# Decode attention with a cached window and a bilinear GLU: x by two rows on ScalarE's queue, and the first weights and K in one load

## The chip, the cores and the metric

The kernel runs on one core of one Trainium2 chip. The metric is the device time of one execution in microseconds, the median of the runs. The profile is one further execution, read by a hardware profiler.

## What is computed

One decoding step for two sequences (B = 2, one token each, D = 512). The input is normalized and goes two ways, and both are added to it:

```python
xn = layernorm(x)
# attention over the last W = 2048 positions of the cache, 32 heads of 128
q = xn @ wq                          # [B, 32, 128]
p = softmax(q . k * 128 ** -0.5)     # k, v: the cache's last 2048 positions
a = (p @ v) @ wo
# GLU without a nonlinearity, F = 1376
f = ((xn @ w_gate) * (xn @ w_up)) @ w_down
y = x + a + f
```

All arrays are float32. K and V of the window are 2 x 32 x 2048 x 128 values each, 67 MB for K and as much for V; with the weights the kernel reads 159 MB for each token pair.

## The kernel before

**The stream.** Everything large lies in one array, `stream`, in the order in which it is needed. `blocks()` (L45) writes that order out: a list of steps, each a list of fields. A field is K of one head with its share of wq (`k`, `wq`), V of one head with its rows of wo (`v`, `wo`), a half of the gate and up weights (`wg`, `wu`), or rows of w_down (`wd`, `wr`). A step holds up to three units of K or V, some 7 MB, as 128 partitions of up to 13,824 words. `pump()` (L143) issues the loads, all on SP's queue, into a ring of three buffers; `done()` (L166) counts the uses of a step's fields, and when the last is done the buffer goes to the next step. SP's issue of that step then waits for the engines that read the old one.

**The small first load.** Ahead of the steps stands a load of 542 words for each partition, into a tile `first` of its own that takes no buffer of the ring: x already laid out by column (`x`, 8 words), the two selection matrices `pick` and `rows` (16 and 6 words), and the part of wq that belongs to head 0 (`w` 0, 512 words). After the three steps that fit the ring SP issues two more small loads: `x_nat`, 16 rows of 128 words with x in the layout of the output, and `carry`, a 9 x 9 matrix that moves accumulator rows.

**Layer norm and projection.** DVE sums x, TensorE spreads the sum over the partitions by a matmul with `mean_w`, the same for the variance, ACT takes the root, and DVE writes `xnb`, the normalized x broadcast over 128 columns (L216 to L234). `project_first(0)` (L245) makes q of head 0 from `w` 0 and `project_first(1)` q of heads 1 to 3 from `w` 1; `project_q` makes the later ones, four heads at a time, while K of earlier heads is used.

**One head.** `products` multiplies K with q on DVE (128 x 4096 words), `sums` adds over the head's 128 columns on DVE, `maxima` and `weights` make the softmax with GpSimd and ACT, `pv` multiplies with V on TensorE into `o_ps`, ACT copies that out, `transpose` turns it with `pick`, ACT scales it into `oT`, and `project_o` adds its product with wo to the accumulator `acc`.

**The accumulator.** `oT` and `hT` have M = 9 columns, of which columns 0 and 8 hold the two sequences (RB = 8), so sequence b stands on accumulator row 8b. The other columns are set to zero once, at the start. For the last heads the 512 columns are split over four row groups of 32 (`accumulate`, L317). The old accumulator is brought there by a matmul of its copy `acc_sb` with `carry` (L496). At the end DVE adds `x_nat` to it (L529), and the 128 x 128 result goes out.

The engines' instructions stay in the order in which they are written (`InOrder`); since that helper records every instruction, nearly all carry line 98 in the profile and are told apart by their tiles.

Of the kernel before, what the change touches and what calls it, by code (L numbers as in the profile page):

```python
# [8 lines left out]
F32 = mybir.dt.float32  # L9
AF = mybir.ActivationFunctionType  # L10
ALU = mybir.AluOpType
# [5 lines left out]
P = 128  # L17
B, D, H, DH, SK, F = 2, 512, 32, 128, 8192, 1376
W = min(4096, max(256, SK // 4))
J = W // P  # L20
NC = D // P
FB = 4 * P
NFB = -(-F // FB)
NFC = F // P
FR = F - NFC * P
FH = [(0, 2 * FB), (2 * FB, F)]
LAG = 3
RB = 8
M = RB * (B - 1) + 1
OUT = P  # L30

CARRY = 72
HG = 4
GC = HG * DH
JG = J // 4
CK, CQ, CO = B * J * DH, NC * GC, D
CP = CQ // NC
UNIT = CK + max(CP, CO)
STEP = 3 * UNIT
WD = [(0, 2), (2, 4), (4, 7), (7, NFC - 1), (NFC - 1, NFC)]  # L40
NS = 3
FX = FR // NS


def blocks():  # L45

    def wd(n):
        return [("wd", i, D) for i in range(*WD[n])]

    def k(h):
        return [("k", h, CK)] + ([("wq", h, CP)] if h + HG < H else [])

    def v(h):  # L60
        return [("v", h, CK), ("wo", h, CO)]

    def gu(half):
        n = NC * (FH[half][1] - FH[half][0])
        return [("wg", half, n), ("wu", half, n)]

    units = []
    for h in range(LAG, H - 1):
        units += [k(h), v(h - LAG)]
    ones = [("pick", 0, 8 * B), ("rows", 0, NFB * B)]  # L70
    first = [("x", 0, B * NC)] + ones + [("w", 0, NC * DH)]
    loads = [[("w", 1, CQ - NC * DH)] + k(0) + k(1), gu(0) + k(2)]
    loads += [gu(1) + units[0] + units[1] + wd(0) + [("wr", 0, NS * P)]]
    loads += [sum(units[i : i + 3], []) for i in range(2, len(units), 3)]
    loads += [k(H - 1) + v(H - 1 - LAG) + wd(1)]
    out = [(("f", 0), first)] + [(("s", i), fields) for i, fields in enumerate(loads)]
    late, last = ("s", len(loads)), ("s", len(loads) + 1)
    out += [(late, v(H - 3)), (late, v(H - 2)), (last, [("v", H - 1, CK)])]
    out += [(last, [("wo", H - 1, CO)] + wd(2))]
    return out + [(last, wd(n)) for n in range(3, len(WD))]  # L80
# [33 lines left out]
def kernel(  # L114
    ctx: ExitStack,
    tc: tile.TileContext,
    x_rows: bass.AP,
    carry_rows: bass.AP,
    stream: bass.AP,
    out: bass.AP,  # L120
):
    nc = tc.nc
    pe, dve, act, sp = (InOrder(tc, e) for e in (nc.tensor, nc.vector, nc.scalar, nc.sync))
    SCALE = float(DH) ** -0.5
    BUFS = 3
# [13 lines left out]
    held = 0  # L139
# [3 lines left out]
    def pump():  # L143
        nonlocal held
        while todo:
            key, fields, at = todo[0]
            if key not in tiles:
                if key[0] == "f":
                    n = sum(w for _, _, w in fields)
                    tiles[key] = const.tile([P, n], F32, name="first")  # L150
                elif held == BUFS:
                    return
                else:
                    held += 1
                    tiles[key] = steps.tile([P, STEP], F32, name="step")
                used[key] = 0
            todo.pop(0)
            c0 = used[key]
            for kind, i, w in fields:
                got[kind, i] = (tiles[key][:, used[key] : used[key] + w], key)  # L160
                used[key] += w
            c1 = used[key]
            src = stream[at : at + P * (c1 - c0)].rearrange("(p i) -> p i", p=P)
            sp.dma_start(tiles[key][:, c0:c1], src)

    def done(kind, i):  # L166
        nonlocal held
        _, key = got.pop((kind, i))
        left[key] -= 1
        if left[key] == 0 and key[0] != "f":  # L170
            del tiles[key]
            held -= 1
            pump()

    pump()
    xT = got["x", 0][0].rearrange("p (b c) -> p b c", b=B)
    pick = got["pick", 0][0].rearrange("p (r s b) -> p r s b", s=2, b=B)
    rows = got["rows", 0][0]

    x_nat = const.tile([P, P], F32, name="x_nat")  # L180
    dve.memset(x_nat, 0.0)
    sp.dma_start(x_nat[::RB, :], x_rows)

    carry = const.tile([P, CARRY], F32, name="carry")[:M, :M]
    sp.dma_start(carry, carry_rows)

    mean_w = const.tile([P, P], F32, name="mean_w")
    dve.memset(mean_w, 1.0 / D)
# [16 lines left out]


    oT_ring = [const.tile([P, M], F32, name=f"oT{i}") for i in range(4)]
    for t in oT_ring:
        nc.gpsimd.memset(t, 0.0)


    tr = ps_c.tile([P, 4 * P], F32, name="tr")
    st = const.tile([P, 4, B], F32, name="st")
    xc = const.tile([P, B, NC], F32, name="xc")
    sq = const.tile([P, B, NC], F32, name="sq")
    dve.tensor_reduce(st[:, 0, :], xT, axis=AX.X, op=ALU.add)  # L216
    pe.matmul(tr[:, 0:B], mean_w, st[:, 0, :], start=True, stop=True)
    dve.tensor_tensor(
# [13 lines left out]
    dve.tensor_copy(  # L232
        xnb, xn.rearrange("p c b -> p (c b)").unsqueeze(2).to_broadcast([P, NC * B, P])
    )  # L234

    q_ps, s_t, mm_t, p_t, sum_t, rec_t, o_sbs, oT = {}, {}, {}, {}, {}, {}, {}, {}
    n_acc = bank = 0
# [108 lines left out]
    def transpose(heads, o_sb):  # L346
        d = tr[:, 8 + 4 * bank : 12 + 4 * bank]
        s0, s1 = side(heads[0]), side(heads[-1]) + 1
        dst = d.rearrange("p (s b) -> p s b", b=B)[:, s0:s1, :]
        for r in range(4):  # L350
            pe.matmul(
                dst, o_sb[:, r * DH : (r + 1) * DH], pick[:, r, s0:s1, :],
                start=(r == 0), stop=(r == 3),
            )
        for h in heads:
            rec = rec_t.pop(h)
            oT[h] = oT_ring[h % 4]
            for b in range(B):
                c = B * side(h) + b
                act.activation(  # L360
                    oT[h][:, RB * b : RB * b + 1], d[:, c : c + 1], AF.Copy,
                    scale=rec[:, b : b + 1],
                )

# [23 lines left out]


    hT = const.tile([P, 4, NFB, M], F32, name="hT")  # L390
    dve.memset(hT, 0.0)

    hX = const.tile([P, NS, M], F32, name="hX")
    dve.memset(hX, 0.0)

    def project_gu(half):
        lo, hi = FH[half]
# [12 lines left out]
    def gate():  # L410
        g_sb = small.tile([P, FB], F32, name="o_sb", bufs=2)
        act.copy(g_sb, gu_ps[0])
        h_sb = small.tile([P, FB], F32, name="o_sb", bufs=2)
        dve.tensor_tensor(h_sb, g_sb, gu_ps[1], op=ALU.mult)
        for i in range(4):
            t = tr[:, P + i * P // 2 : P + i * P // 2 + NFB * B]
            pe.matmul(t, h_sb[:, i * P : (i + 1) * P], rows, start=True, stop=True)
            act.copy(hT[:, i, :, ::RB], t.rearrange("p (n b) -> p n b", b=B))
        for i in range(NS):
            t = tr[:, P + (2 * i + 1) * P // 4 : P + (2 * i + 1) * P // 4 + NFB * B]  # L420
            f = (NFC % 4) * P + i * FX - FR
            pe.matmul(t, h_sb[:, f : f + P], rows, start=True, stop=True)
            act.copy(hX[FR:, i, ::RB], t[FR:, (NFB - 1) * B :])

    def down(n):
        for c in range(*WD[n]):
# [62 lines left out]
    down(1)  # L489

    acc_sb = const.tile([M, D], F32, name="acc_sb")
    dve.tensor_copy(acc_sb, acc)
    sums(h + 1)
    transpose([HF], o_sb)
    keep_busy(256)
# [30 lines left out]
    down(3)  # L526
    down(4)
    o_out = const.tile([P, P], F32, name="o_out")
    dve.tensor_tensor(o_out, acc_g, x_nat, op=ALU.add)  # L529

    sp.dma_start(out, o_out[:OUT, :])

# [1 line left out]
def laid_out(x):  # L534
# [1 line left out]
    import numpy as np  # L536

    a = x["A_x"].reshape(B, D)
    first = {
        kind: np.zeros((P, w), a.dtype) for kind, _, w in blocks()[0][1][:3]  # L540
    }
    carry = np.zeros((M, M), a.dtype)
    first["x"][:] = a.reshape(B, P, NC).transpose(1, 0, 2).reshape(P, B * NC)
    for b in range(B):
        for r in range(4):
            for s in range(2):
                first["pick"][8 * s + 4 * b + r :: 32, (2 * r + s) * B + b] = 1.0
        for n in range(NFB):
            first["rows"][32 * n + b, n * B + b] = 1.0
        carry[RB * b, RB * b] = 1.0  # L550
    cache = {
        kind: x[name][:, :, SK - W :, :].reshape(B, H, P, J * DH).transpose(1, 2, 0, 3)
        for kind, name in (("k", "A_k_cache"), ("v", "A_v_cache"))
# [8 lines left out]
    rest = wd[NFC * P :].reshape(FR, NS + 1, P)  # L562

    def field(kind, i):
        if kind in first:
            return first[kind]
        if kind in ("k", "v"):
            return cache[kind][i].reshape(P, CK)
        if kind == "w":
            return (wq[0][:, :, DH:] if i else wq[0][:, :, :DH]).reshape(P, -1)  # L570
        if kind == "wq":
            return wq[i // HG + 1][:, i % HG, :]
        if kind == "wo":
            return wo[i]
        if kind == "wr":
            last = rest[:, NS, :].reshape(NS, FX, P).swapaxes(0, 1)
            return np.concatenate([rest[:, :NS, :], last]).reshape(P, NS * P)
        if kind == "wd":
            return wd[i * P : (i + 1) * P]
        return gu[kind][:, :, FH[i][0] : FH[i][1]].reshape(P, -1)  # L580
# [2 lines left out]
        np.concatenate([field(kind, i) for kind, i, _ in fields], axis=1).ravel()  # L583
        for _, fields in blocks()
    ]
    x_rows = np.zeros((D // P, 32 // RB, P), a.dtype)
    x_rows[:, :B] = a.reshape(B, D // P, P).transpose(1, 0, 2)
    return {
        "x_rows": x_rows.reshape(-1, P),
        "carry": carry,  # L590
        "stream": np.concatenate(parts),
    }

# [31 lines left out]
```

## Time and profile before

| what | value |
|---|---|
| median of 3 runs | 377.54 us (377.41 to 377.73) |
| profiled execution, span from first to last instruction | 375.7 us |
| median less that span | 1.84 us |
| bytes read | 159.47 MB |
| mean rate over the span | 425 GB/s |
| busy, PE / DVE / ACT / POOL | 256.5 / 294.6 / 58.7 / 25.3 us |

The profile holds the span of the profiled execution, not a device time of its own; the median of the runs stands beside it. The rows of the profile name an engine, an operation, the tile written and the tiles read, with start and duration in microseconds; `128*9` in a matmul is the shape of the stationary operand. PEld is TensorE's load of weights, SPq the queue of SP. "DMA share" in a table of windows is the mean busy share of the 16 DMA engines; a packet is counted where it starts, so a short window can show more than 1.

### The profile page before, as it was taken

To read this page: it belongs to the slowest core of one execution; us is meant where nothing else is said; L and a number is where in the kernel's file an instruction comes from. 1 tells how busy PE (TensorE), PEld (TensorE's weight loads), DVE (VectorE), ACT (ScalarE), POOL (GpSimd) and SP (SyncE) were. 2 spreads that over 40 slices of the span, in tenths; PEclk is the share of its full clock that TensorE was granted. 3 is DMA by queue.
4 is the path that set the end of the run, shared out by engine and by line. 5 is a ranking of instruction groups with operands and counts; after the bars stand their busy time and mean duration, and the time that the engine had idled before them with its cause. 6 is when DMAs were issued, how large, how long until landed. Compare 5 with 4: busy or idle time off the path is not lost.

```text
span 375.7 us, 2891 instructions
## 1 busy us (share of the span) xinstructions
PE 256.5 (68%) x1100; PEld 88.1 (23%) x1100; DVE 294.6 (78%) x147; ACT 58.7 (16%) x259; POOL 25.3 (7%) x78
## 2 busy tenths in 40 slices
PE   3396696986548487864848676485867639637996
PEld 3241122331112122211222211121212213021334
DVE  3299691998599499769949976994996799599960
ACT  1021001122020211201112020111202011121131
POOL 1001000000000000100000100000000000000010
PEclk9796988899696966859686786976669887556999
DMA  8999999899999999999999999999999999999995
GB/s 327 463 436 454 408 426 471 383 465 432 414 465 394 459 424 424 461 400 453 418 437 449 412 447 424 432 442 430 436 436 424 437 434 436 436 425 424 419 421 226
DMA packets 4382, 159.70 MB, mean 425 GB/s; under 512 B 514, under 2 KB 658, under 8 KB 1042
## 3 DMA queue, kind: packets, MB, share of 16 engines
q1 hardware_dynamic: 4370, 159.54, 98.5%
q8 instruction: 8, 0.13, 0.1%
q14 instruction: 4, 0.03, 0.0%
HBM read 159.47 MB, written 0.07 MB: 425 GB/s over the span
## 4 chain that ended last, share of the span: by engine, by line
DMA 62%; DVE 29%; PE 7%; ACT 1%; issue 0%; SPq 0%; DVEq 0%
DMA step<-in_stream_dram 62%; DVE s L98 14%; DVE step L98 14%; PE o_ps L98 3%; PE q L98 2%; PE acc L98 2%; PE tr L98 1%; DVE m L98 0%; ACT o_sb L98 0%; ACT oT L98 0%; SPq L98 0%; DVE rec L98 0%; DVE o_out L98 0%; DVEq L98 0%
## 5 line engine op out<-in xcount | busy, mean ns | idle before, releaser
L98 DVE TENSOR_TENSOR step<-step,q 128x4096 f32<-128x4096 f32 x31 | 136.6, 4408 | 53.3 <-DMA step<-in_stream_dram 53.3
L98 PE MATMUL q<-step,xnb 128*128 128x512 f32 (+1 forms) x128 | 92.7, 874 | 75.5 <-DMA step<-in_stream_dram 75.5
L98 DVE TENSOR_REDUCE s<-step 128x32 f32<-128x4096 f32 x32 | 141.4, 4419 | 1.1
L98 PE MATMUL o_ps<-step,p 128*16 128x512 f32 (+1 forms) x512 | 69.7, 682 | 10.3 <-DMA step<-in_stream_dram 10.3
L98 PEld LDWEIGHTS q<-step,xnb 128*128 128x128 f32 x128 | 32.2, 275 | 128.9 <-DMA step<-in_stream_dram 79.1
L98 PE MATMUL acc<-step,oT 128*9 128x512 f32 (+1 forms) x88 | 35.2, 554 | 9.3 <-ACT oT L98 8.1
L98 PE MATMUL tr<-first,o_sb 128*128 128x2 f32 (+2 forms) x198 | 27.6, 258 | 15.3 <-ACT o_sb L98 12.8
L98 ACT COPY o_sb<-o_ps 128x512 f32<-128x512 f32 (+1 forms) x24 | 13.8, 576 | 143.1 <-PE o_ps L98 143.1
L98 PEld LDWEIGHTS tr<-first,o_sb 128*128 128x128 f32 x198 | 25.5, 196 | 37.3 <-ACT o_sb L98 32.6
L295 POOL PARTITION_ALL_REDUCE mm<-m x32 | 11.3, 354 | 283.4 <-DVE rec L98 178.9
L98 PEld LDWEIGHTS o_ps<-step,p 128*16 128x16 f32 x512 | 13.5, 106 | 70.4 <-issue 55.2
L98 ACT ACTIVATE nm<-mm 128x2 f32<-128x2 f32 x32 | 6.5, 203 | 129.5 <-POOL mm L295 129.5
L98 ACT ACTIVATE p<-s,nm 128x16 f32<-128x16 f32 x64 | 19.2, 300 | 1.0
L98 ACT ACTIVATE oT<-tr,rec 128x1 f32<-128x1 f32 x64 | 12.2, 260 | 28.3 <-PE tr L98 28.3
L311 POOL PARTITION_ALL_REDUCE sum<-rs x32 | 12.7, 398 | 54.8 <-ACT p L98 54.8
L98 PE MATMUL o_ps<-step,xn 128*2 128x512 f32 (+1 forms) x48 | 12.9, 593 | 0.0
L98 ACT ACTIVATION_READ_ACCUMULATOR p<-s,nm 128x1 f32 x64 | 12.0, 187 | 0.0
L98 DVE TENSOR_TENSOR step<-step,tr 128x4096 f32<-128x4096 f32 x1 | 4.4, 4421 | 9.3 <-DMA step<-in_stream_dram 9.3
L98 PEld LDWEIGHTS acc<-step,oT 128*9 128x9 f32 x88 | 4.3, 91 | 19.5 <-ACT oT L98 13.1
L98 PE MATMUL q<-xnb,mean_w 128*128 128x512 f32 (+1 forms) x18 | 8.5, 563 | 0.0
L98 PE MATMUL acc<-step,hT 128*9 128x128 f32 (+2 forms) x58 | 7.9, 357 | 0.0
L98 DVE TENSOR_REDUCE m<-s 128x2 f32<-128x32 f32 x32 | 5.9, 186 | 1.1
(43 smaller groups left out, 36.5 us busy)
## 6 DMA issues: line engine op xcount, KB each, us to landing
step<-in_stream_dram SPq DMA_DIRECT2D x16, 6912.0 KB, 33.7
step<-in_stream_dram SPq DMA_DIRECT2D x2, 6400.0 KB, 32.6
step<-in_stream_dram SPq DMA_DIRECT2D x1, 6720.0 KB, 45.6
step<-in_stream_dram SPq DMA_DIRECT2D x1, 6656.0 KB, 28.9
step<-in_stream_dram SPq DMA_DIRECT2D x1, 5376.0 KB, 15.4
step<-in_stream_dram SPq DMA_DIRECT2D x1, 4864.0 KB, 30.1
step<-in_stream_dram SPq DMA_DIRECT2D x2, 2304.0 KB, 17.2
step<-in_stream_dram SPq DMA_DIRECT2D x1, 2048.0 KB, 15.9
```

The lines of the kernel that those rows point to most:

```text
L98: made = call(*args, **kwargs)
L295: nc.gpsimd.partition_all_reduce(mm, m, P, bass_isa.ReduceOp.max)
L311: nc.gpsimd.partition_all_reduce(sum_t[h], rs, P, bass_isa.ReduceOp.add)
```

## The change

- The small first load goes. Its selection matrices (now one field `ones`) and head 0's part of wq stand at the head of the first step, ahead of `w` 1 and K of heads 0 and 1. That step has 11,286 words for each partition, where it had 10,752.
- x comes as `x_own`, two rows of 512 words with a 2 x 2 unit matrix beside them, by a load that ScalarE issues as its first instruction. Four small matmuls with that unit matrix turn it into `xT`, which DVE copies out of PSUM; the layer norm goes on from there.
- ACT copies `pick` and `rows` from the first step into a tile of their own (`ones`), so that the step's buffer can be given back.
- M is 2: `oT` and `hT` have one column for each sequence, there is nothing to set to zero, and accumulator row b is sequence b. `x_nat` and the separate `carry` are gone, with their loads; `carry` is the unit matrix that came with x.
- x is added to the accumulator where it is copied to `acc_sb`, on two rows; the last step on DVE is a copy of `acc_g`.

On SP's queue the three steps that fit the ring are now the first three instructions, and the next one is the load that waits for the first buffer. ACT's queue begins with the load of x. On PE the projection of head 0 waits for the first step.

```diff
-RB = 8
-M = RB * (B - 1) + 1
+M = B
...
-    ones = [("pick", 0, 8 * B), ("rows", 0, NFB * B)]
-    first = [("x", 0, B * NC)] + ones + [("w", 0, NC * DH)]
-    loads = [[("w", 1, CQ - NC * DH)] + k(0) + k(1), gu(0) + k(2)]
+    first = [("ones", 0, ONES), ("w", 0, NC * DH), ("w", 1, CQ - NC * DH)]
+    loads = [first + k(0) + k(1), gu(0) + k(2)]
...
-    out = [(("f", 0), first)] + [(("s", i), fields) for i, fields in enumerate(loads)]
+    out = [(("s", i), fields) for i, fields in enumerate(loads)]
...
+    x_own = const.tile([P, D + M], F32, name="x_own")[:M, :]
+    act.dma_start(x_own, x_rows)
+    x_own, carry = x_own[:, :D].rearrange("m (c p) -> m c p", c=NC), x_own[:, D:]
+
     pump()
-    xT = got["x", 0][0].rearrange("p (b c) -> p b c", b=B)
...
-    x_nat = const.tile([P, P], F32, name="x_nat")
-    dve.memset(x_nat, 0.0)
-    sp.dma_start(x_nat[::RB, :], x_rows)
-
-    carry = const.tile([P, CARRY], F32, name="carry")[:M, :M]
-    sp.dma_start(carry, carry_rows)
...
+    xT = const.tile([P, B, NC], F32, name="xT")
+    for c in range(NC):
+        pe.matmul(tr[:, 16 + B * c : 16 + B * c + B], x_own[:, c, :], carry, start=True, stop=True)
+    dve.tensor_copy(xT, tr[:, 16 : 16 + B * NC].rearrange("p (c b) -> p b c", b=B))
     dve.tensor_reduce(st[:, 0, :], xT, axis=AX.X, op=ALU.add)
...
+    act.copy(ones, got["ones", 0][0])
+    done("ones", 0)
...
-    dve.tensor_copy(acc_sb, acc)
+    dve.tensor_tensor(
+        acc_sb.rearrange("m (p c) -> m p c", c=NC), acc.rearrange("m (p c) -> m p c", c=NC),
+        x_own.rearrange("m c p -> m p c"), op=ALU.add,
+    )
...
-    dve.tensor_tensor(o_out, acc_g, x_nat, op=ALU.add)
+    dve.tensor_copy(o_out, acc_g)
```

More of the change, by code (lines that the diff above doesn't have):

```diff
@@ L27 @@
 LAG = 3
-RB = 8
-M = RB * (B - 1) + 1
+M = B
 OUT = P
-CARRY = 72
 HG = 4
@@ L42 @@
 FX = FR // NS
+ONES = 8 * B + NFB * B
 def blocks():
@@ L117 @@
     x_rows: bass.AP,
-    carry_rows: bass.AP,
     stream: bass.AP,
@@ L147, in pump @@
             if key not in tiles:
[L148 to L151, printed above, removed]
+                if held == BUFS:
                     return
-                else:
-                    held += 1
-                    tiles[key] = steps.tile([P, STEP], F32, name="step")
+                held += 1
+                tiles[key] = steps.tile([P, STEP], F32, name="step")
                 used[key] = 0
@@ L169, in done @@
         left[key] -= 1
-        if left[key] == 0 and key[0] != "f":
+        if left[key] == 0:
             del tiles[key]
@@ L173, in done @@
             pump()
+    x_own = const.tile([P, D + M], F32, name="x_own")[:M, :]
+    act.dma_start(x_own, x_rows)
+    x_own, carry = x_own[:, :D].rearrange("m (c p) -> m c p", c=NC), x_own[:, D:]
     pump()
-    xT = got["x", 0][0].rearrange("p (b c) -> p b c", b=B)
-    pick = got["pick", 0][0].rearrange("p (r s b) -> p r s b", s=2, b=B)
-    rows = got["rows", 0][0]
-    x_nat = const.tile([P, P], F32, name="x_nat")
-    dve.memset(x_nat, 0.0)
-    sp.dma_start(x_nat[::RB, :], x_rows)
-    carry = const.tile([P, CARRY], F32, name="carry")[:M, :M]
-    sp.dma_start(carry, carry_rows)
+    ones = const.tile([P, ONES], F32, name="ones")
+    pick = ones[:, : 8 * B].rearrange("p (r s b) -> p r s b", s=2, b=B)
+    rows = ones[:, 8 * B :]
     mean_w = const.tile([P, P], F32, name="mean_w")
@@ L207 @@
     oT_ring = [const.tile([P, M], F32, name=f"oT{i}") for i in range(4)]
-    for t in oT_ring:
-        nc.gpsimd.memset(t, 0.0)
     tr = ps_c.tile([P, 4 * P], F32, name="tr")
@@ L360, in transpose @@
                 act.activation(
-                    oT[h][:, RB * b : RB * b + 1], d[:, c : c + 1], AF.Copy,
+                    oT[h][:, b : b + 1], d[:, c : c + 1], AF.Copy,
                     scale=rec[:, b : b + 1],
@@ L390 @@
     hT = const.tile([P, 4, NFB, M], F32, name="hT")
-    dve.memset(hT, 0.0)
     hX = const.tile([P, NS, M], F32, name="hX")
-    dve.memset(hX, 0.0)
     def project_gu(half):
@@ L417, in gate @@
             pe.matmul(t, h_sb[:, i * P : (i + 1) * P], rows, start=True, stop=True)
-            act.copy(hT[:, i, :, ::RB], t.rearrange("p (n b) -> p n b", b=B))
+            act.copy(hT[:, i, :, :], t.rearrange("p (n b) -> p n b", b=B))
         for i in range(NS):
@@ L422, in gate @@
             pe.matmul(t, h_sb[:, f : f + P], rows, start=True, stop=True)
-            act.copy(hX[FR:, i, ::RB], t[FR:, (NFB - 1) * B :])
+            act.copy(hX[FR:, i, :], t[FR:, (NFB - 1) * B :])
     def down(n):
@@ L538, in laid_out @@
     a = x["A_x"].reshape(B, D)
[L539 to L543, printed above, removed]
+    ones = np.zeros((P, ONES), a.dtype)
     for b in range(B):
@@ L546, in laid_out @@
             for s in range(2):
-                first["pick"][8 * s + 4 * b + r :: 32, (2 * r + s) * B + b] = 1.0
+                ones[8 * s + 4 * b + r :: 32, (2 * r + s) * B + b] = 1.0
         for n in range(NFB):
-            first["rows"][32 * n + b, n * B + b] = 1.0
-        carry[RB * b, RB * b] = 1.0
+            ones[32 * n + b, 8 * B + n * B + b] = 1.0
     cache = {
@@ L564, in field @@
     def field(kind, i):
-        if kind in first:
-            return first[kind]
+        if kind == "ones":
+            return ones
         if kind in ("k", "v"):
@@ L585, in laid_out @@
     ]
-    x_rows = np.zeros((D // P, 32 // RB, P), a.dtype)
-    x_rows[:, :B] = a.reshape(B, D // P, P).transpose(1, 0, 2)
     return {
-        "x_rows": x_rows.reshape(-1, P),
-        "carry": carry,
+        "x_rows": np.concatenate(
+            [a.reshape(B, P, NC).swapaxes(1, 2).reshape(B, D), np.eye(M, dtype=a.dtype)], axis=1
+        ),
         "stream": np.concatenate(parts),
@@ L623 @@
     y = r.results[0]["out_0_dram"]
-    return y[[32 * g + RB * b for b in range(B) for g in range(D // P)]].reshape(B, 1, D)
+    return y[[32 * g + b for b in range(B) for g in range(D // P)]].reshape(B, 1, D)
```

## The prediction

> **What bounds the kernel now.** I read the page first (share of the engines, DMA queues), then the chain that ended last, then busy time by windows, then the first 75 us of the timeline and the SP queue, then the tail.
>
> ```profile
> span 375.7 us, 2891 instructions
> q1 hardware_dynamic: 4370, 159.54, 98.5%
> DMA 62%; DVE 29%; PE 7%; ACT 1%; issue 0%; SPq 0%; DVEq 0%
> ```
>
> The second line is the load queue: its packets occupied the 16 DMA engines for 98.5% of the whole span. The third is the chain that ended last; its 29% of DVE must not be read as a bound by DVE, since a piece of it ends each time in a load that had long been queued behind others. The windows decide it (columns: stretch, length, busy time of PE, PEld, DVE, ACT, POOL, granted clock, DMA share, GB/s):
>
> ```profile
> 0.00:1.70 1.70, 0.00 (x0) 0.00 (x0) 0.78 (x4) 0.98 (x1) 1.17 (x14) 1.00 0.00 0
> 1.70:2.82 1.12, 0.00 (x0) 0.00 (x0) 0.99 (x3) 0.30 (x1) 0.08 (x3) 1.00 0.87 197
> ...
> 15.60:371.30 355.70, 250.18 (x1032) 82.80 (x1036) 290.68 (x131) 56.84 (x256) 24.09 (x64) 0.79 1.00 432
> 371.30:372.20 0.90, 0.90 (x44) 0.80 (x37) 0.00 (x0) 0.30 (x2) 0.00 (x0) 1.00 0.35 134
> 372.20:374.00 1.80, 0.75 (x24) 0.21 (x12) 0.29 (x1) 0.00 (x0) 0.00 (x0) 1.00 0.00 0
> ```
>
> Between 15.6 and 371.3 us the DMA share is 1.00 at 432 GB/s, while DVE is busy 290.68 of 355.70 us and PE less. The kernel is one uninterrupted stream: 159.54 MB at 432 GB/s are 369.3 us. Around it stand 1.7 us before the first byte, a slow start, and about 3.5 us after the last (372.2 to 375.7). A change moves the time if it moves the start of the stream, its bytes or rate, its tail, or if it lets the queue run dry.
>
> The span is 375.7 us and the median of the runs 377.54; the 1.84 us around the span are taken as unchanged, so a change of the span is carried over to the median one for one. Measurement of this kernel can tell about 0.2%, 0.75 us, from no change.
>
> **The loads, where the change is made.** Start, duration, SP's own queue; then the same loads by size and time to landing:
>
> ```profile
> 0.72 0.37 SPq L98 DMA_DIRECT2D first<-in_stream_dram  x1
> 1.15 1.37 SPq L98 DMA_DIRECT2D step<-in_stream_dram  x3
> 2.56 0.55 SPq L98 DMA_DIRECT2D x_nat<-in_x_rows_dram  x1
> 3.15 0.54 SPq L98 DMA_DIRECT2D carry<-in_carry_dram  x1
> 34.56 0.35 SPq L98 DMA_DIRECT2D step<-in_stream_dram  x1
> ...
> 43.61 0.33 SPq L98 DMA_DIRECT2D step<-in_stream_dram  x1
> ...
> 73.14 0.33 SPq L98 DMA_DIRECT2D step<-in_stream_dram  x1
> ```
>
> ```profile
> step<-in_stream_dram SPq DMA_DIRECT2D x1, 6720.0 KB, 45.6
> ...
> step<-in_stream_dram SPq DMA_DIRECT2D x1, 5376.0 KB, 15.4
> first<-in_stream_dram SPq DMA_DIRECT2D x1, 271.0 KB, 2.9
> x_nat<-in_x_rows_dram SPq DMA_DIRECT2D x1, 8.0 KB, 45.3
> ```
>
> *Bytes.* The small load's 271 KB go into the first step, less 4 KB for x (8 columns of 128 rows). x_nat (8 KB) and carry (0.3 KB) go, x_own (2 rows of 514 words, 4.1 KB) comes. That is 8.2 KB less, 0.02 us at 432 GB/s.
>
> *Row size.* 128 rows of 2,168 bytes become part of 128 rows of 45,144. Near the end only rows of 8 KB and less are moved:
>
> ```profile
> 368.30:370.00 1.70, 1.70 (x33) 0.72 (x25) 0.00 (x0) 0.37 (x1) 0.00 (x0) 1.00 0.96 401
> ```
>
> 271 KB (0.278 MB) are 0.69 us at 401 GB/s and 0.64 at 432: 0.05 us saved.
>
> ```profile
> 372.55 0.12 PEld L98 LDWEIGHTS acc<-step,hT 128*9 128x9 f32 x8 [0.25 <-DMA step<-in_stream_dram]
> ```
>
> *Start.* SP's first issue stands at 0.72 as before. In 1.70:2.82 the engines were 0.87 busy but moved 197 GB/s, 0.22 MB where the stream rate gives 0.48: the slow start costs 0.26 MB, 0.6 us. Busy engines that move little are waiting for their first reads, and whichever load stands first pays that; I take 0.0. If it belonged to the short rows, 0.6 us would be saved, and by another count 1.0: the first step landed at 1.15 + 15.4 = 16.55, while 5.78 MB from 1.70 on at 432 GB/s end at 15.1, 1.4 earlier, of which some 0.4 is the way from a last byte (372.2 in the windows) to the weight load that waited for it (372.55). On the other side a load of 43 KB rows has never been first in this trace: the first step was issued at 1.15 and moved after 2.82, at most 1.7 us later, where the small load took 1.0 (0.72 to 1.70); so up to 0.7 us could be lost. The nearer row is the small load's, same engine, same place.
>
> The Trainium skill, "DMA: Bandwidth & Descriptors", section "Anatomy of one DMA — SWDGE (gpsimd) path", gives every DMA about 2.0 us of fixed cost beside its bytes, on the GpSimd path; read as a price for each load, one load fewer would give an estimate of 375.5 us. The trace speaks against it: three loads stand back to back from 1.15 on and the share stays 1.00, so such a cost is latency that overlaps.
>
> *x on ScalarE's queue.* x_own is issued by ACT at about 0.72, on a queue of its own. x_nat, behind three steps in SP's queue, needed 45.3 us; the small load, with nothing ahead, 2.9. I take 2.9 to 5. The same page, section "Queues, rings and completion order", says that each DMA engine takes turns between queues, one packet at a time, so a row on ScalarE's queue would wait for a packet or so and not for the steps; no run here shows it yet.
>
> **The first head.** Start, duration, what ended the idle time before:
>
> ```profile
> 3.64 0.16 DVE L98 TENSOR_REDUCE st<-first 128x2 f32<-128x8 f32 x1 [0.84 <-DMA first<-in_stream_dram]
> 6.42 0.69 DVE L98 COPY xnb<-xn 128x1024 f32<-128x1024 f32 x1
> 7.21 3.46 PE L98 MATMUL tr<-first,xnb 128*128 128x128 f32 x16 [1.53 <-issue]
> 16.60 4.42 DVE L98 TENSOR_TENSOR step<-step,tr 128x4096 f32<-128x4096 f32 x1 [9.34 <-DMA step<-in_stream_dram]
> 47.68 4.42 DVE L98 TENSOR_TENSOR step<-step,q 128x4096 f32<-128x4096 f32 x1 [3.85 <-DMA step<-in_stream_dram]
> ```
>
> From x's landing to xnb took 3.5 us (3.64 to 7.11). The transpose adds four matmuls and a copy; two such single-pass matmuls, on mean_w, hold PE for 1.2 us in all, so four for 2.4 at most, and the copy 0.16:
>
> ```profile
> L98 PE MATMUL tr<-st,mean_w 128*128 128x2 f32 x4 | 1.2, 363 | 4.5 <-DVE st L98 4.5
> ```
>
> With x at 5.0, xnb stands at 5 + 2.6 + 3.5 = 11.1, before the step's landing at about 16.4. Hidden by that load, 5 us to spare.
>
> But the projection of head 0 (tr<-first, 3.46 us) needs w, and w now lands with K at 16.4. DVE's first product, at 16.60 before, waits for it; queued behind on PE is the projection of heads 1 to 3, which waited for this same load before. And PE has then idled:
>
> ```profile
> 14.00:16.00 2.00, 0.00 (x0) 0.00 (x0) 0.00 (x0) 0.00 (x0) 0.00 (x0) 0.50 1.51 651
> ```
>
> The granted clock is 0.50 there against 1.00 at 7.21, so the 3.46 us become up to 6.9; I take 5.5. The Trainium skill, "TensorE: Matmul & The Clock Gate", "What's actually happening", says the same of idle time: half clock after an idle window of some 3.4 us, back after as long a busy one. By it the estimate is 3.4 us at half speed, then full: about 5.2.
>
> So DVE starts some 5 us later (3.3 to 6.7). Who is late next? SP's issue at 34.56 waits for the buffer of step 0: it moves to 39.6. The queue then still holds what landed at 47.6 (the DVE row at 47.68 ends its wait there): 13 us of cover before, 8 after. At 47.68 DVE had idled 3.85 us, which takes up most of the shift, leaving 1.2. The next tight issue is the one at 73.14; the queue then holds the two steps issued at 34.56 and 43.61, the later landing 37.9 us after its issue:
>
> ```profile
> step<-in_stream_dram SPq DMA_DIRECT2D x1, 6912.0 KB, 37.9
> ```
>
> that is at 81.5, 8.4 us later; less about 1.0 to 1.7 from issue to first byte, 6.7 are spare against 1.2. The step that lands at 65.2 finds DVE idle (below), and there the shift is gone. Cost: 0.
>
> ```profile
> 65.19 4.42 DVE L98 TENSOR_TENSOR step<-step,q 128x4096 f32<-128x4096 f32 x1 [7.88 <-DMA step<-in_stream_dram]
> ```
>
> **The rest.** Memsets of x_nat, hT, hX and oT go (DVE and POOL wait for loads then), ACT's copy of pick and rows comes, and waits for step 0; queued behind it is only the first nm, some ten us later. Rows M fall from 9 to 2:
>
> ```profile
> L98 PEld LDWEIGHTS acc<-step,hT 128*9 128x9 f32 x56 | 1.9, 91 | 3.7 <-issue 3.4 <-DMA step<-in_stream_dram 0.3
> L98 PEld LDWEIGHTS o_ps<-step,xn 128*2 128x2 f32 x48 | 2.7, 88 | 11.6 <-issue 11.6
> L98 DVE COPY acc_sb<-acc 9x512 f32<-9x512 f32 x1 | 0.7, 672 | 0.0
> L98 DVE TENSOR_TENSOR o_out<-acc,x_nat 128x128 f32<-128x128 f32 x1 | 0.3, 292 | 8.2 <-PE acc L98 8.2
> ```
>
> A load of 2 columns costs 88 ns where 9 cost 91: nothing. acc_sb becomes a sum of the same 512 elements, some 0.68 for 0.67, 15 us before the end. The last o_out becomes a copy, on the path; by the copy's 672 ns for 512 elements, 128 of them are about 0.2 to 0.29: 0.0 to 0.1 saved, I take 0.05.
>
> **Sum.** 0.02 + 0.05 + 0.0 + 0.05 = about 0.1 us less: span 375.6, median 377.4. With the start's bounds (1.0 saved, 0.7 lost) the range of the forecast is 376.4 to 378.1.
>
> **Rivals.**
> *The slow start belonged to the short rows* (faster). For: 0.87 busy at 197 GB/s while only those were moved. Against: the first bytes come late whatever the load. If it goes with the separate issue, 0.6 to 1.0 come off beside the 0.1: 376.4 to 376.8, on both sides of the bound of 0.2%, say 376.6.
> *x is late and the queue runs dry* (slower). The place is the issue at 34.56. Each us that DVE's first product is later than about 11 us after 16.6 (3.85 + 6.7 of cover) is a us of idle DMA; that is x landing after 15.6 (15.6 + 2.6 + 3.5 + 5.5 = 27.2). Were it served behind the three steps, like x_nat at 45.3, x lands at 46, the first product runs at 57.6, 41 us late, step 0 is given back at 75.6, 28 us after the queue ran empty: 405 us. For: x_nat's row. Against: another queue, issued at the same time as the first step.
> *The long unaligned rows are slower* (slower). Rows of 45,144 bytes are no multiple of 512, those of 43,008 are. At the 401 GB/s of the short rows the 5.78 MB take 14.4 us for 13.4: 378.4. It decides below 409 GB/s. Against: nothing in the trace shows such rows losing rate.
> *The change frees nothing because the first bytes come when they came*: that is the forecast without its 0.1, 377.5.
>
> **Chances.** Forecast, with nothing freed, 0.70; short rows 0.18, of which 0.14 past the bound; x late 0.04; long rows 0.05; the loss of a late start, with the 0.7 at its full size, 0.03. So faster by over 0.2% 0.14, within 0.2% 0.74, slower 0.12. Range 376.5 to 378.1, the start's bounds but for the last 0.1.
>
> **What would show it.** Right: DMA share 1.00 and 432 GB/s from 16 to 371 us; x_own landed by 6 us, the first product at 20 to 23, the issue that stood at 34.56 now near 39.6, product of head 4 again at its landing near 65. Wrong: a stretch with a share under 0.95 between 40 and 90 us, x_own landing after 15 us, first bytes later than 2.4 us or the first step landing before 15.9 or after 17.

## The result, and the profile after

| kernel | median us | runs | against before |
|---|---|---|---|
| before | 377.54 (377.30 to 377.73) | 5 | |
| changed | 378.88 (378.70 to 379.07) | 5 | 1.0039 (95%: 1.0027 to 1.0050) |

The change costs 1.34 us. The forecast was 377.4, no change, with a range up to 378.1.

The page of the changed kernel, its load queue and its chain:

```profile
span 377.2 us, 2895 instructions
q1 hardware_dynamic: 4176, 159.53, 98.3%
q10 hardware_dynamic: 4, 0.00, 0.0%
DMA 62%; PE 21%; DVE 14%; ACT 1%; issue 1%; SPq 0%; DVEq 0%
```

The span grew by 1.5 us for the same bytes; the load queue is as full as before. q10 is ScalarE's queue with the two rows of x. The shares of PE and DVE in the chain changed places, which only says who waited beside a DMA that was never idle.

The same stretches as in the prediction:

```profile
0.00:1.70 1.70, 0.00 (x0) 0.00 (x0) 0.72 (x4) 0.41 (x1) 1.10 (x10) 1.00 0.01 2
15.60:371.30 355.70, 251.12 (x1032) 84.95 (x1032) 291.15 (x131) 56.53 (x255) 24.09 (x64) 0.79 1.00 431
372.20:374.00 1.80, 1.80 (x56) 1.45 (x59) 0.00 (x0) 0.41 (x2) 0.00 (x0) 1.00 0.31 120
```

The share between 15.6 and 371.3 us is 1.00 again, so the queue never ran dry; but the rate reads 431 GB/s where it read 432, and the stream is still moving after 372.2, where it had ended. One GB/s in 432 is 0.8 us of 356, as near as whole GB/s can tell. That is the first half of the loss, in a digit that is easily passed over.

The first loads, by size and time to landing:

```profile
step<-in_stream_dram SPq DMA_DIRECT2D x1, 6720.0 KB, 47.8
step<-in_stream_dram SPq DMA_DIRECT2D x1, 6400.0 KB, 31.3
step<-in_stream_dram SPq DMA_DIRECT2D x1, 5643.0 KB, 16.5
x_own<-in_x_rows_dram ACTq DMA_DIRECT2D x1, 4.0 KB
```

The first step was issued at 0.72 and landed at 17.2; before, issued at 1.15 it landed at 16.55. Both had moved the same 5.78 MB by then. 0.65 us are lost in the first load: the second half.

Products that waited for a load, and the last issue, in the timeline of the changed kernel:

```profile
17.39 3.76 PE L96 MATMUL tr<-step,xnb 128*128 128x128 f32 x16 [11.05 <-DMA step<-in_stream_dram]
21.19 4.42 DVE L96 TENSOR_TENSOR step<-step,tr 128x4096 f32<-128x4096 f32 x1 [13.42 <-PE tr L96]
39.22 0.33 SPq L96 DMA_DIRECT2D step<-in_stream_dram  x1
49.48 4.42 DVE L96 TENSOR_TENSOR step<-step,q 128x4096 f32<-128x4096 f32 x1 [1.05 <-DMA step<-in_stream_dram]
65.82 4.42 DVE L96 TENSOR_TENSOR step<-step,q 128x4096 f32<-128x4096 f32 x1 [6.37 <-DMA step<-in_stream_dram]
75.98 0.33 SPq L96 DMA_DIRECT2D step<-in_stream_dram  x1
326.44 4.42 DVE L96 TENSOR_TENSOR step<-step,q 128x4096 f32<-128x4096 f32 x1 [4.24 <-DMA step<-in_stream_dram]
374.72 0.35 SPq L96 DMA_DIRECT2D out_dram<-o_out  x1
```

Two rows of the kernel before that answer to the last two:

```profile
325.15 4.42 DVE L98 TENSOR_TENSOR step<-step,q 128x4096 f32<-128x4096 f32 x1 [4.00 <-DMA step<-in_stream_dram]
...
373.34 0.35 SPq L98 DMA_DIRECT2D out_dram<-o_out  x1
```

The product of head 4 waits for its load in both kernels, at 65.19 and 65.82: 0.63 later. The product near 326 stands 1.29 later, the issue of the output 1.38. So 0.63 are lost before 65 us, 0.66 creep in over the next 260, and the tail adds 0.1.

### The profile page after: what moved, and what is told of

Read it like the earlier page. It is cut to its first block, busy times and chain, and to the rows that moved or that the text cites. A ratio compares the mean times of both kernels' runs of the same rounds, so it can differ in the third digit from the quotient of the medians.

```text
span 377.2 us, 2895 instructions
## 1 busy us (share of the span) xinstructions
PE 257.2 (68%) x1108; PEld 90.0 (24%) x1108; DVE 294.9 (78%) x145; ACT 58.9 (16%) x260; POOL 25.2 (7%) x74
## 4 chain that ended last, share of the span: by engine, by line
DMA 62%; PE 21%; DVE 14%; ACT 1%; issue 1%; SPq 0%; DVEq 0%
DMA step<-in_stream_dram 62%; PE o_ps L96 8%; DVE s L96 7%; DVE step L96 7%; PE q L96 5%; PE acc L96 4%; PE tr L96 3%; ACT o_sb L96 0%; ACT oT L96 0%; SPq L96 0%; DVE o_sb L96 0%; ACT hT L96 0%; DVE m L96 0%; ACT hX L96 0%; DVE o_out L96 0%
## 5 line engine op out<-in xcount | busy, mean ns | idle before, releaser
L96 PE MATMUL q<-step,xnb 128*128 128x512 f32 (+1 forms) x128 | 91.2, 861 | 68.0 <-DMA step<-in_stream_dram 68.0
L96 PE MATMUL o_ps<-step,p 128*16 128x512 f32 (+1 forms) x512 | 70.6, 690 | 10.6 <-DMA step<-in_stream_dram 10.6
L96 PE MATMUL acc<-step,oT 128*2 128x512 f32 (+1 forms) x88 | 34.6, 546 | 9.1 <-ACT oT L96 9.1
L96 PE MATMUL tr<-ones,o_sb 128*128 128x2 f32 (+2 forms) x198 | 28.4, 262 | 15.2 <-ACT o_sb L96 12.8
L96 PEld LDWEIGHTS tr<-ones,o_sb 128*128 128x128 f32 x198 | 26.3, 201 | 37.2 <-ACT o_sb L96 32.7
L96 PE MATMUL tr<-step,xnb 128*128 128x128 f32 x16 | 3.8, 429 | 11.1 <-DMA step<-in_stream_dram 11.1
L96 PEld LDWEIGHTS acc<-step,oT 128*2 128x2 f32 x88 | 3.7, 83 | 19.0 <-ACT oT L96 14.5
L96 PE MATMUL acc<-step,hT 128*2 128x128 f32 (+2 forms) x58 | 7.9, 356 | 0.0
```

What stands on the lines that cost most here:

```text
L96: made = call(*args, **kwargs)
```

## The experiments

Each ran beside the kernel before on the same chip, which gave 377.30 to 377.35; the differences below are to that. The ratios with their 95% intervals, about 0.0009 or 0.35 us each way, are not the quotients of the medians and can differ from them by up to 0.0005. Each kernel has one trace. The theories, as the expectations name them: *address* (where the ring of step buffers begins in SBUF, the memory that the loads write to), *start* (what the first load's rows cost, later divided into *unaligned rows* and *long first row*, or *uneven start*), *queue* (the load on ScalarE's queue), *late head* (head 0's projection, now after the first step).

What the address theory rests on: in the built kernels the three buffers begin at bytes 30,720, 86,016 and 141,312 of each partition before, all multiples of 512, and at 29,376, 84,672 and 139,968 after, 192 over. The tiles ahead of the ring had shrunk by 1,344 bytes. In the kernel before, the `carry` tile is 72 words wide and uses 9.

**e1: the ring back on its address.**

```diff
-    x_own = const.tile([P, D + M], F32, name="x_own")[:M, :]
+    x_own = const.tile([P, D + M + 336], F32, name="x_own")[:M, : D + M]
```

> The changed kernel with 336 unused words behind x_own in SBUF, so that the ring of three step buffers begins at byte 30,720 of each partition (a multiple of 512, as before the change) instead of 29,376 (192 over a multiple of 512). Address theory (rows written to a ring off the 512 grid are a little slower all through the stream): most long rows go back from 2.044 to 2.051 us to 2.041, the stream ends some 0.6 us earlier, about 378.2 against 378.9 for the change. Start theory (only the long rows of the first load lose time): 378.9, with the first step landing at 17.2 as in the change. Queue theory (the load on ScalarE's queue slows the stream): 378.9, rows still at 2.044 and more. Late-head theory (the late projection of head 0): 378.9.

378.02 us, 1.0020 (1.0011 to 1.0029), +0.69. Timeline and loads:

```profile
65.61 4.42 DVE L96 TENSOR_TENSOR step<-step,q 128x4096 f32<-128x4096 f32 x1 [6.65 <-DMA step<-in_stream_dram]
325.54 4.42 DVE L96 TENSOR_TENSOR step<-step,q 128x4096 f32<-128x4096 f32 x1 [4.22 <-DMA step<-in_stream_dram]
```

```profile
step<-in_stream_dram SPq DMA_DIRECT2D x1, 5643.0 KB, 16.3
```

From 65.61 to 325.54 are 259.93 us, as before the change (259.96; changed 260.62). The first load still lands late, at 17.0.

**e2: the kernel before with the ring off its address.**

```diff
-CARRY = 72
+CARRY = 120
```

> The kernel before with 48 unused words more behind carry, so that the ring begins at 30,912, 192 over a multiple of 512; nothing else is changed. Address theory: most long rows take 2.044 to 2.051 us, about 378.2 against 377.5. Start, queue and late-head theories: 377.5, no change.

378.23 us, 1.0021 (1.0012 to 1.0030), +0.90. Forty-eight unused words slow a kernel that is otherwise untouched; the start, queue and late-head theories can't give that. The first load lands as before (1.15 + 15.5), and by the product near 326 us part of the delay is there: 260.38 us after the product of head 4, where it was 259.96.

```profile
step<-in_stream_dram SPq DMA_DIRECT2D x1, 5376.0 KB, 15.5
```

```profile
65.25 4.42 DVE L98 TENSOR_TENSOR step<-step,q 128x4096 f32<-128x4096 f32 x1 [6.73 <-DMA step<-in_stream_dram]
325.63 4.42 DVE L98 TENSOR_TENSOR step<-step,q 128x4096 f32<-128x4096 f32 x1 [4.24 <-DMA step<-in_stream_dram]
```

The packet records of the traces, for the 2,048 rows of 55,296 bytes that make most of the stream (the mean without the few over 2,060 ns):

```
kernel            ring, over a multiple of 512   rows at 2,041 ns   median   mean
before                          0                     1,947          2,041   2,041.2
changed                       192                       521          2,044   2,044.6
e1                              0                     2,033          2,041   2,041.0
e2                            192                       460          2,044   2,044.8
e7                            256                     1,973          2,041   2,041.2
e8                             64                       335          2,044   2,045.0
```

Each DMA engine moves 159.5 MB / 16, as much as 180 such rows; 3.4 ns on each are 0.6 us.

**e7 and e8: which grid,** that is, on a multiple of how many bytes a buffer has to begin. CARRY = 136 and CARRY = 88 in the kernel before.

> The kernel before with the ring at 30,976, 256 bytes over a multiple of 512. If the grid that counts is 512 bytes: 378.2, as with 192 over. If it is 256 or less: 377.3, rows at 2.041 us.

> The kernel before with the ring at 30,784, 64 bytes over a multiple of 512. If the grid that counts is 64 bytes: 377.3. If it is 128 or more: 378.2, as with 192 over, which is also a multiple of 64; that run leaves 64 unlikely already, so 378.2 is what I expect.

e7: 377.36 us, 0.9995 (0.9986 to 1.0004). e8: 378.16 us, 1.0019 (1.0010 to 1.0028), +0.81. 64 and 192 over a multiple of 256 lose, and a multiple of 256 that is none of 512 does not. No run has a buffer 128 over, so the grid may be 256 bytes or 128.

**e3: the small load back, all else as changed.**

```diff
-    loads = [first + k(0) + k(1), gu(0) + k(2)]
+    loads = [first[2:] + k(0) + k(1), gu(0) + k(2)]
...
-    out = [(("s", i), fields) for i, fields in enumerate(loads)]
+    out = [(("s", 0), first[:2])] + [(("s", i), fields) for i, fields in enumerate(loads)]
```

> The changed kernel with the selection matrices and head 0's part of wq as a small load of their own again (534 words, into the same buffer), issued ahead of the rest of the first step; x still comes by ScalarE and the ring still begins at 29,376. Start theory: the first step lands some 0.6 us earlier, about 378.3 against 378.9. Late-head theory: all of it comes back, 377.5. Address theory alone and queue theory: 378.9.

378.28 us, 1.0026 (1.0017 to 1.0035), +0.95. The step behind the small load lands as before, at 1.15 + 15.3:

```profile
step<-in_stream_dram SPq DMA_DIRECT2D x1, 5376.0 KB, 15.3
step<-in_stream_dram SPq DMA_DIRECT2D x1, 267.0 KB, 2.8
```

What is left is the address's 0.8 to 0.9. It is 0.39 better than the change.

**e4: both edits.**

> Both of these edits on the changed kernel: the small load of its own and the ring at 30,720. Address and start theories together: about 377.5, level with the kernel before. Queue theory: 378.9. Late-head theory: 377.5, as with the small load alone.

377.36 us, 1.0000 (0.9991 to 1.0009). Both losses are gone, with x on ScalarE's queue, M = 2 and all the rest of the change in place but the merged first load, and with it the late head. The queue theory falls. The ring is worth 0.65 (changed to e1) to 0.92 (e3 to e4), the first load 0.39 (changed to e3) to 0.69 (e1 to e4), and both 1.34 together; the two values of each differ by less than the intervals.

**e5: rows of the first load on the 512 grid.** The `ones` field is padded from 22 to 128 words; one load, ring at 30,720.

> The changed kernel with the ring at 30,720 (378.02 as measured) and the field with the selection matrices padded from 22 to 128 words, so that the rows of the first load are 45,568 bytes, a multiple of 512, instead of 45,144; one load as in the change. The padding adds 54 KB, 0.13 us. Unaligned-rows theory (rows that are no multiple of 512 bytes are read slower): the first step lands some 0.4 to 0.6 us earlier, about 377.6. Long-first-row theory (the engines start badly when the first row of each is long): no change but the padding, 378.1.

378.15 us, 1.0016 (1.0007 to 1.0025), +0.80, of which 0.13 are the padding. No gain in time, against the unaligned-rows theory. The load still lands at 0.72 + 16.6:

```profile
step<-in_stream_dram SPq DMA_DIRECT2D x1, 5696.0 KB, 16.6
```

**e6 and e9: x later, without and with the aligned rows.** The load of x stands behind a one-column root in ScalarE's program. The traces show its issue at 1.03, ahead of the root (2.01) and not at 2.3; but its two rows moved only at 5.66 and 6.21 in e6 (5.79 and 6.04 in e9), where the changed kernel has them at 1.65 and 1.67, just ahead of the first step's. So SP's first rows had the DMA engines to themselves, as was wanted.

> The changed kernel with the ring at 30,720 and the load of x issued by ScalarE after its table load and a one-column root, at about 2.3 us instead of 0.72, so that SP's first issue has the DMA engines to itself. Queue theory (the simultaneous issue on ScalarE's queue delays the first rows, which started between 1.7 and 2.6 us): the first step lands 0.4 to 0.6 us earlier, about 377.5. Long-first-row and unaligned-rows theories: 378.0.

> Two earlier edits together: rows of 45,568 bytes in the first load and x issued at about 2.3 us; ring at 30,720, one load. With the rows on the 512 grid alone the other engines finished the first step at 16.1 on average, but one that began late finished at 16.9 and ended the stream last. If the load of x is what holds that engine up (queue theory): 377.6, the first step lands at 16.4. If long first rows start unevenly in any case (long-first-row theory): 378.1 and a late engine again.

e6: 378.00 us, 1.0016 (1.0005 to 1.0027). e9: 378.19 us, 1.0023 (1.0013 to 1.0033). The load of x has no part in the loss.

**e10: rows of 45,312 bytes, x later.**

> The same with rows of 45,312 bytes, a multiple of 256 and not of 512. If the grid for rows in memory is 256 bytes, as it is for the ring: rows at their shortest time with no gaps between them, as with 45,568, and 0.06 us less to move. If it is 512: gaps between rows again, the engines' mean end of the first step 0.4 us later, about 378.0.

377.90 us, 1.0019 (1.0010 to 1.0028), +0.60. The engines' mean end is 15.98, so its rows run as in e9 (16.09, with 0.03 MB more); the slowest engine and the time stay late.

**e11: unaligned rows away from the start.** A field of 22 unused words behind the second step of the kernel before.

> The kernel before with 22 unused words behind the fields of the second step, so that its rows are 51,288 bytes, 88 over a multiple of 256, in the middle of the stream and away from its start; 11 KB more, 0.03 us. Unaligned-rows theory: that step takes some 0.4 us more, 377.8. If only the start of the stream matters: 377.4.

377.37 us, 1.0005 (0.9997 to 1.0014). A miss for the unaligned-rows theory: rows 88 bytes over a multiple of 256 in memory took 1.894 us for 51,288 bytes, those of 51,200 took 1.891, and the 88 bytes more are worth that difference.

**e12: a very small load first.** `ones` alone, padded to 512 bytes a row.

> The changed kernel with the ring at 30,720 and the selection matrices (128 words a row, padded) as a load of their own ahead of the first step; head 0's part of wq stays in the first step, whose rows are now 45,056 bytes, a multiple of 512, and x is issued by ScalarE at 0.72 as in the change. Long-first-row theory (a short first row evens the start out): first step lands at 16.5, 377.5. Late-head theory: 378.1, since head 0's projection still waits for the first step. Queue theory: 378.1.

378.00 us, 1.0018 (1.0010 to 1.0027), +0.70. A miss: a load of short rows ahead is not enough by itself. (The execution that was traced took 378.31.)

```profile
step<-in_stream_dram SPq DMA_DIRECT2D x1, 5632.0 KB, 16.4
step<-in_stream_dram SPq DMA_DIRECT2D x1, 64.0 KB, 1.8
```

**e13: all of the first wq ahead, rows of 8,448 bytes; and e14: the small load padded to 2,304-byte rows.**

> The changed kernel with the ring at 30,720 and the selection matrices (64 words a row, padded) with all of the first wq as a load of their own ahead of K: rows of 8,448 bytes (1.08 MB), then rows of 36,864 bytes. x is issued at 0.72 as in the change. Uneven-start theory (one or two engines get their first row up to 0.8 us late, where all get it within 0.3 us when the first rows are short; with long rows the late one never catches up): 377.5, the first step lands at 16.5. If only rows of 2 KB do it: 378.0.

> The small load of its own again, padded to 576 words, so that its rows are 2,304 bytes and the first step's fields behind it begin on a multiple of 256 bytes in the buffer too; ring at 30,720. Uneven-start theory: 377.4, as with 534 words; the offset inside one step's buffer is worth 0.05 us at most and the padding costs as much. It is also the version that could beat both kernels, by no more than 0.2 us.

e13: 377.31 us, 1.0004 (0.9994 to 1.0014). e14: 377.38 us, 1.0004 (0.9995 to 1.0013). Rows of 8 KB ahead repair the start as rows of 2 KB do:

```profile
step<-in_stream_dram SPq DMA_DIRECT2D x1, 4608.0 KB, 15.3
step<-in_stream_dram SPq DMA_DIRECT2D x1, 1056.0 KB, 4.8
```

The packet records of the start, in us; "long" is the first row of each of the 16 engines that is over 36 KB, "ideal" its size at the rate of later rows, the last columns are the engines' ends of the first step:

```
kernel    first rows   first starts   long starts, mean   took   ideal   end, mean   end, last
before       2,168      1.72 to 1.98        3.01          1.78   1.59      15.91       16.20
changed     45,144      1.73 to 2.56        1.98          2.35   1.67      16.54       16.95
e4           2,136      1.72 to 2.05        2.92          1.85   1.59      15.89       16.23
e5          45,568      1.74 to 2.76        1.99          2.39   1.68      16.15       16.94
e10         45,312      1.71 to 2.52        1.87          2.40   1.67      15.98       16.57
e12            512      1.72 to 1.82        2.70          2.26   1.66      16.60       17.27
e13          8,448      1.72 to 2.38        5.03          1.37   1.36      15.92       16.11
```

Long rows that start at 1.9 to 2.7 on the mean take 0.6 to 0.7 us more than their ideal; at 2.9 to 3.0, 0.2 to 0.3; at 5.0, nothing. Single rows spread more: in the changed kernel the one that started at 1.84 took 1.34 more, the one at 2.56 took 0.14 more. With rows of 45 KB first, the first 16 rows also start up to 1.0 us apart; in e13 they start 0.66 apart and nothing is lost, so an uneven start alone doesn't explain it. In e12 the 64 KB were through before the long rows began, at 2.2 to 3.6 us, and these met the same slow start.

A step lands with its last engine, and the lead of the others is not shared out later: in e5 the stream's last engine ended at 372.68, the next at 372.04, the mean at 371.61. (The records don't name the engines, so that it is the one that began last is argued, not shown.) This is also why e5 and e10 gained nothing. Their rows, on a multiple of 256 bytes, did bring the engines' mean end of the first step from 16.47 (e1) to 16.15 (e5) and from 16.34 (e6) to 15.98 (e10), and, by the same records, the mean end of the stream from 371.98 to 371.61 and from 372.00 to 371.59; but the last engine ended at 372.68 in e5 and 372.33 in e10, against 372.45 and 372.46. So far as one trace each can tell, the unaligned-rows theory is right about the mean at the start of the stream and wrong about the time.

No kernel separates the late head from the start by its time alone, since a short load that carries head 0's part of wq repairs both. The traces do: the first step's landing at 17.2 stands ahead of the late head and can't be its effect, and the DMA share of 1.00 behind it leaves no idle time for it to have caused. In e1, with the late head and the ring on its address, 48.6 us pass from that landing (17.0) to the product of head 4 and 259.93 from there to the product near 326; before, with an early head, it was 48.6 (from 16.55) and 259.96.

## Why the prediction was wrong

**The bound** held: one stream with a DMA share of 1.00, and only its start, bytes, rate and tail count. All of the loss but the tail's 0.1 is in start and rate, the two terms that the sum had at nothing; the 0.02 of bytes and 0.05 of row size are less than the runs can tell.

**The start** was the term that was mis-sized. It was taken as 0.0, between 1.0 saved and 0.7 lost, with the reasons that "whichever load stands first pays that" and that the small load's row was the nearer one. The runs show 0.65 of landing time lost, 0.39 to 0.69 of the whole; the landing at 17.2 is one of the signs of being wrong that the prediction had named. Whichever load stands first does pay, but not the same: at the later rows' pace the 5.78 MB, eight rows of 1.667 us for each engine, would end at 15.06 from 1.72 on, and the engines' mean end was 15.91 before and 16.54 after. The load that was called nearer had rows of 2 KB, and the new first load has rows of 45 KB. The bound of 0.7 fits in size by luck: it was worked out as a later first byte, and the first rows start at 1.73 us as they did at 1.72; what is late is their end. What makes long rows slow there no run shows.

**The rate** had no term for where the buffers lie. The sum took 432 GB/s as given; the smaller `const` tiles moved the ring by 1,344 bytes, and that alone is 0.65 to 0.92 us. The rival of slower rows was near in kind but wrong in place: it looked at the rows in memory (45,144 bytes, no multiple of 512), which e11 shows to cost nothing within the stream, and not at the address in SBUF. The Trainium skill, "DMA: Bandwidth & Descriptors", section "How a descriptor splits into AXI transactions", says that a transfer that doesn't begin on a 256-byte boundary begins with a transaction from the boundary below, and that the bytes in between still cost beats of 32 bytes. It says so of reading; the ring is the side that is written. Carried over to the ring, an estimate from it is 6 beats of a row's 1,728, 7 ns, for 192 over and 2 beats, 2.4 ns, for 64 over; 3.4 to 3.6 and 3.8 were measured. So the boundary agrees with e7 and e8, and the sizes don't. On the side that is read, e11 shows no such cost.

**The late head** came as worked out, and hid as worked out: the first product at 21.19 (20 to 23 was forecast), the fourth step's issue at 39.22 (39.6), head 4's product again at its landing. Its size, 4.6 us where some 5 was forecast, was right by luck. The projection was expected to slow from 3.46 to 5.5 us by an idle clock, and took 3.76; another 0.8 came from its start at 17.39, behind the late first load. Weight loads of both kernels, by tile:

```profile
L98 PEld LDWEIGHTS tr<-first,xnb x16: 192/333/337, 7.2 to 10.3; 128*128 128x128 f32 x16
```

```profile
L96 PEld LDWEIGHTS tr<-step,xnb x16: 288/333/338, 17.4 to 20.5; 128*128 128x128 f32 x16
```

The median was 333 ns already at 7.2 us, where later ones take 190: the projection before ran at that slow pace too, though the granted clock read 1.00 from 6 to 10 us. The changed kernel reads 1.00 from 14 to 20 us, where 0.50 was read before, so the forecast of a slower projection rested on a reading that the weight loads don't bear out.

**x on ScalarE's queue** landed by 2.19, ahead of the 2.9 to 5 assumed. Its two rows moved before the first step's, so the changed kernel doesn't show what a row waits beside a full queue. e6 does: issued 0.31 us later, x landed by 8.33.

```profile
2.19 1.78 PEld L96 LDWEIGHTS tr<-x_own 2*128 2x128 f32 x8 [2.19 <-DMA x_own<-in_x_rows_dram]
```

```profile
1.03 0.56 ACTq L96 DMA_DIRECT2D x_own<-in_x_rows_dram  x1
8.33 1.77 PEld L96 LDWEIGHTS tr<-x_own 2*128 2x128 f32 x8 [8.33 <-DMA x_own<-in_x_rows_dram]
```

That is later than the range: the rows moved from 5.66 on, behind some two of the step's (which took 2.25 and 1.68 us on the mean from 1.72 on), and not behind three steps as x_nat did; the turns between queues of the Trainium skill, "DMA: Bandwidth & Descriptors", section "Queues, rings and completion order", cited in the prediction, agree with that, but for two packets where one was expected. The rival of a late x didn't come, and at 8.33 x is still hidden by the first step.

**The tail**: the copy of o_out took 0.29 us as the sum had, so the 0.05 were not saved.

```profile
373.94 0.11 PEld L96 LDWEIGHTS acc<-step,hT 128*2 128x2 f32 x8 [0.24 <-DMA step<-in_stream_dram]
374.40 0.29 DVE L96 COPY o_out<-acc 128x128 f32<-128x128 f32 x1 [7.90 <-PE acc L96]
```

The sum into acc_sb, put at 0.68, took 1.02 us, and PE waited 0.3 us for it:

```profile
L96 DVE TENSOR_TENSOR acc_sb<-acc,x_own x1: 1021/1021/1021, 358.1 to 358.1; 2x512 f32<-2x512 f32 x1
```

## What to carry to other kernels

Where a kernel is one long stream of loads, write down where its buffers begin: an edit that resizes any tile allocated ahead of them moves them, and 64 or 192 bytes off a multiple of 256 each long row here lost some 0.2%. Open the stream with a load of short rows that keeps the long ones back for a microsecond or more (0.27 MB in rows of 2 KB and 1.08 MB in rows of 8 KB did, 0.06 MB did not) and let the long rows follow. In such a kernel the remaining edits, here x's route and M, may be made for their own sake: e4 and e13 are level with the kernel before, and no version beat it.

## What the runs showed of the hardware that was not expected

Buffers 64 or 192 bytes over a multiple of 256 in SBUF slowed most rows of 55,296 bytes from 2,041 to 2,044 to 2,051 ns; 256 over a multiple of 512 did not, and 128 over was not run. First rows of 45 KB took 2.35 us where later ones take 1.67, and the first rows started up to 1.0 us apart. Two rows on ScalarE's queue landed by 2.19 us when issued at 0.72, beside SP's first load, and by 8.33 when issued at 1.03. Weight loads took 333 ns while the granted clock read 1.00.
